# Start-up fills, first loads and delay terms of a planned two-layer kernel: one variant in place of another

## The chip, the cores and the metric

One core of one Trainium2 chip runs the whole program. The metric is the device time of one execution in microseconds (us): the median of several runs. A run of this kernel is told from another at about 0.2%, some 3.7 us.

The core has five instruction streams that run beside each other and wait for each other through semaphores: TensorE (PE in the profile: matmuls; PEld: its weight loads), VectorE (DVE), ScalarE (ACT), GpSimd (POOL) and SyncE (SP, which here only issues DMA transfers). Each stream is executed strictly in the order in which it was written.

## The reference, cut to what matters

Two layers are applied twice in turn to x (2048 tokens x 512): A is attention over segments of 32 tokens with a memory of 8 tokens that is handed from segment to segment, B is a gated feed-forward layer. Both passes use the same weights.

```
def _A_ref(x, mem0, Wq, Wk, Wv, Wo, seg_len):     # 32 heads of 128, M = 8
    mem = mem0
    for s in range(n_seg):                         # 64 segments of 32 tokens
        h = concatenate([mem, x[segment s]])       # 40 rows
        q, k, v = h @ Wq, h @ Wk, h @ Wv           # per head
        p = softmax(where(mask, q @ k.T * scale, -1e9))
        o = (p @ v) summed over heads through Wo
        mem = o[:, :M]                             # memory of the next segment
        outs.append(o[:, M:])
def _B_ref(x, w_gate, w_up, w_down):
    return (sigmoid(x @ w_gate) * (x @ w_up)) @ w_down
x = x + _A_ref(_layernorm(x), ...)
x = x + _B_ref(_layernorm(x), ...)
x = x + _A_ref(_layernorm(x), ...)
x = x + _B_ref(_layernorm(x), ...)
```

Segment s+1 needs the memory that segment s leaves, so layer A is a chain of 64 steps; the feed-forward layer and the V projections of tokens that are already known hang on no such chain.

## The kernel before, in words

**Steps.** The kernel runs 70 steps (`emit_step`). Step t treats segment t of the first pass of layer A (job 0) and segment t-6 of the second pass (job 1) together, where both exist: steps 0 to 5 have job 0 alone (40 rows), steps 6 to 63 have both (80 rows), steps 64 to 69 have job 1 alone. In a step the 32 heads go in units of 3 heads and groups of 6 (the last of 2). For each unit: Q and K by matmuls with `wq`, `wk` (L721), a copy to `qku`, scores (L735). For each group: the softmax (L748 to L780: mask, maximum, subtraction, exponential on ACT, sum, reciprocal, product into `pb`), a transpose by matmul (L794), a copy to `ptsb`, P times V (L807), a copy to `otsb`, Wo (L824). After the last head the 8 memory rows go into `hT` of the next step (L837, or L842 with one job).

**V.** V of the x tokens is made ahead in passes of 128 rows (`v_pass`, L583): eight pieces of 512 columns, copied to a staging tile and stored to a scratch tensor in DRAM (`scr`); each step loads its 24 rows from there (L681). A store with fewer than 24 tokens per segment is rearranged so that the token is its outermost dimension (8 or 16) and the segment the next. The remaining 32 rows of each step (the memory and the newest tokens) are projected in the step itself (`add_strips`, L693), copied in two halves to `sst`, and moved to `vsb` by four DMAs (L702). Nine V passes, 288 matmuls of 512 columns, belong to the start (`v_group`); the others come with the feed-forward blocks.

**Start.** `setup_consts` makes the identity, the masks and small constants. `clear` plans the zero fills of `hT`, `pb` and `vsb` and the small `maskb` transfer. Then come the loads of x blocks, of the initial memory (`load_mem0`) and of the weights (`load_weights`), about 18 MB. Layer norm (`layernorm_T`) is on DVE except for the power -1/2, which POOL computes (L542).

**What sets the order.** All work is entered as tasks with an engine, a duration and what it reads and writes (`Planner.add`). `plan` orders the tasks of each engine by list scheduling with these durations, with a latency from each engine to those that wait for it (`gap`), and with places in rotating buffers; it also chooses between ACT and DVE for tasks that name both. `late` adds a term to the latency from a TensorE task to the task that has it: -980 ns for the copy of the first strip half, +40 ns for the `qku` copy, +240 ns for the copy into `oxT`. The order found is then written out. So a change of an assumed duration or latency can move instructions anywhere in the program. Early loads carry a `boost` that sets their order; the SP queue waits, at each DMA, for the DMA eight places earlier.

Of the kernel before, what the change touches and what calls it, by code (L numbers as in the profile page):

```python
# [16 lines left out]
P = 128  # L17
MEM = 8
SEG = 32
L = MEM + SEG  # L20
LW = 2 * L
# [5 lines left out]
BLK = 4  # L27
# [24 lines left out]
class Task:  # L52
    __slots__ = ("eng", "dur", "lat", "fn", "deps", "succ", "tail", "boost", "ndep", "ready", "start", "idx", "on", "fresh", "acq", "rel", "durs", "tick", "prev", "land", "adj")

    def __init__(self, eng, dur, lat, fn, boost):
        self.durs = dur if isinstance(dur, dict) else {e: dur for e in eng}
        self.eng, self.dur, self.lat, self.fn, self.boost = eng, min(self.durs.values()), lat, fn, boost
        self.deps, self.succ, self.fresh = set(), [], set()
        self.acq, self.rel = [], []
        self.on = None  # L60
        self.land = 3000.0
        self.adj = {}
# [21 lines left out]
class Planner:  # L84
# [18 lines left out]
    def add(self, eng, dur, fn, r=(), w=(), lat=None, boost=0.0, use=(), late=0.0):  # L103
# [18 lines left out]
        if late:  # L122
            tk.adj = {d: late for d in tk.fresh if self.tasks[d].eng == ("PE",)}
# [6 lines left out]
    def gap(self, a, b):  # L130

        d = b.adj.get(a.idx, 0.0)
        if a.eng == b.eng:
            return a.lat if a.eng[0] in ("DVE", "ACT", "SP") or len(a.eng) > 1 else 0.0
        return a.lat + d + (self.TO_PE if b.eng[0] == "PE" else 0.0)
# [211 lines left out]
class Kern:  # L347
# [103 lines left out]
    def setup_consts(self):  # L451
        nc, tc = self.nc, self.tc
        cmasks.make_identity(nc, self.ident[:])
# [5 lines left out]
        nc.gpsimd.memset(self.mask1[0:MEM, :], 0.0)  # L459
        nc.gpsimd.affine_select(out=self.maskb[0:L, 0:SEG], in_=self.maskb[0:L, 0:SEG], pattern=[[-1, SEG]],  # L460
# [6 lines left out]

    def clear(self):

        nc, pl = self.nc, self.pl  # L470
        pl.add("SP", 430, lambda: nc.sync.dma_start(out=self.maskb[L:LW, :], in_=self.mask1[:]), w=["maskb"])
        for k, t_ in enumerate(self.hT):
            pl.add("DVE", 120, lambda t_=t_: nc.vector.memset(t_[:, :, L:2 * L], 0.0), w=[("hT", k, 1, q) for q in ("m", "x")])
        for k, t_ in enumerate(self.pb):
            pl.add("DVE", 400, lambda t_=t_: nc.vector.memset(t_[:], 0.0), w=[("pb", k)])
        for k, t_ in enumerate(self.vsb):
            keys = [("vs", k), ("vx", 0, k), ("vx", 1, k)]
            if k == 0:
                pl.add("DVE", 550, lambda t_=t_: nc.vector.memset(t_[:], 0.0), w=keys)
            else:  # L480
                pl.add("ACT", 960, lambda t_=t_: nc.scalar.copy(out=t_[:], in_=self.vsb[0][:]), r=[("vs", 0)], w=keys)

    def load_weights(self):
# [9 lines left out]
        xb = list(self.boot_x)[1:]  # L493
        for h0, n in ((0, 4), (4, 4), (8, 8), (16, 8), (24, 8)):
            cs = slice(h0 * P, (h0 + n) * P)
            ld(self.wv[:, :, cs], wv_v[:, :, cs], P * self.DC * n * P * 2 / 300.0, [("wv", h) for h in range(h0, h0 + n)])
            if h0 == 0:
                continue
            for b in xb[:3]:
                self.load_x(b, *self.boot_x[b])  # L500
            xb = xb[3:]
        for g, (h0, gsz, us) in enumerate(self.groups):
            cs = slice(h0 * P, (h0 + gsz) * P)
            nb = P * self.DC * gsz * P * 2
            for nm, sb, v in (("wq", self.wq, wq_v), ("wk", self.wk, wk_v)):
                ld(sb[:, :, cs], v[:, :, cs], nb / 300.0, [(nm, h) for h in range(h0, h0 + gsz)])
            ld(self.wo[:, h0:h0 + gsz, :], wo_v[:, h0:h0 + gsz, :], P * gsz * self.D * 2 / 300.0, [("wo", h) for h in range(h0, h0 + gsz)])
# [6 lines left out]
    def load_mem0(self):  # L514
        nc, pl, DC = self.nc, self.pl, self.DC
        m0 = self.xo[0][0:MEM, :]
        pl.add("SP", 100, lambda: nc.sync.dma_start(out=m0, in_=self.mem0), w=[("xo", 0)], lat=2500.0, boost=self.boot())
# [114 lines left out]
    def pre1(self, b):  # L632
        nc, pl = self.nc, self.pl
        i = self.nxt("xs", self.NX)
        xb = self.xs[i]
        pl.add("SP", 430, lambda: nc.sync.dma_start(out=xb[:], in_=self.x_in[b * P:(b + 1) * P, :]), w=[("xs", i)], lat=2500.0 if b < 2 else None, boost=(self.boot() if b < 2 else 0))
# [12 lines left out]
    def emit_step(self, t):  # L649
# [34 lines left out]
        def add_strips(col, lo, key):  # L684
# [13 lines left out]
            for q in range(2):  # L698
                pl.add(("ACT", "DVE"), copy_ns(512), lambda q=q: (sb[:, q, :], vb[q][:, :]), r=[vb[q]], w=[(sb, q)], use=[sb], late=-980.0 * (q == 0))
# [7 lines left out]
        for g, (h0, gsz, us) in enumerate(self.groups):  # L707
            hs = slice(0, gsz)
            SB = pl.buf(self.bank)
            for u in us:  # L710
# [20 lines left out]
                pl.add("ACT", act_ns(2 * nh * ncol, True), qkcopy, r=[pq], w=[qku], late=40.0)  # L731
# [12 lines left out]
            for idx, j in reversed(list(enumerate(jobs))):  # L744
# [6 lines left out]
                    r=[SB] + ([("st", gi, 0)] if both and j == 0 else []) + (["maskb"] if both else []), w=[("st", gi, 0), ("st", gi, 1)])  # L751
# [92 lines left out]
        for idx, j in enumerate(jobs):  # L844
# [4 lines left out]
            pl.add("ACT", 160, lambda dst=dst, a=48 * j - c0: (dst, wo3(a, SEG)), r=[WB], w=[("oxT", j, oi, s % BLK)], late=240.0)  # L849
# [120 lines left out]
    def trace(self):  # L970
        self.fill = {}
        self.lw = None
        self.clear()
# [7 lines left out]
        self.load_x(2, *self.boot_x[2])  # L981
        self.load_mem0()
# [20 lines left out]
    def run(self):  # L1003
        nc = self.nc
        self.setup_tiles()
        self.trace()
        order = self.pl.plan()
        with self.tc.manual_schedule():
            self.setup_consts()
# [67 lines left out]
```

## Time and profile before

| quantity | before |
|---|---|
| time, median of 3 runs | 1860.91 us (1858.97 to 1861.75) |
| profiled execution: time, span | 1860.91 us, 1859.1 us |
| PE busy | 1818.1 us (98%) |
| DVE, ACT, POOL busy | 1274.6 us (69%), 1173.8 us (63%), 571.8 us (31%) |
| granted TensorE clock, mean | 0.996 |
| HBM traffic over the span | 134 GB/s |

The profile describes one execution, of 1860.91 us, whose span between the first and the last instruction is 1859.1 us; 1.8 us lie around it. Busy time is the time in which an engine has at least one instruction running. Idle time of an engine is put down to what ended it ("<-"). Matmuls overlap in TensorE's pipeline, so the distance from one start to the next, not the length of one, is their cost.

### The profile page before, as it was taken

Reading aid. Unit: us, or ns where it says so; the run is one execution under the profiler, and the core shown is the slowest. Engines: PE = TensorE matmul, PEld = TensorE weight load, DVE = VectorE, ACT = ScalarE, POOL = GpSimd, SP = SyncE. Lnnn points to the kernel's source line nnn. Section 1 sums busy time; section 2 is a strip of 40 time slices with the busy share of each in tenths; the row PEclk is TensorE's granted clock in tenths of the full one; section 3 lists DMA queues with packets and bytes.
Section 4 is the critical chain, followed back from the end, with each engine's and each line's share of the span. In section 5 each row is a group of like instructions: output and inputs, shape, how many; then the busy total and the mean of one; then the engine's idle time right before and its main releaser. Section 6 shows DMA issues by size and latency. Waiting matters only on the chain.

```text
span 1859.1 us, 94041 instructions
## 1 busy us (share of the span) xinstructions
PE 1818.1 (98%) x41066; PEld 1577.1 (85%) x41282; DVE 1274.6 (69%) x4115; ACT 1173.8 (63%) x2748; POOL 571.8 (31%) x821
## 2 busy tenths in 40 slices
PE   7999999999999999999999999999999999999998
PEld 3678788889888898989888888989888888988787
DVE  5456566776677667767677777767677666767565
ACT  6665666666666666666666656666666666665553
POOL 4215023322424142323424142323424142324223
PEclk9999999999999999999999999999999999999999
DMA  9626234444645454554645364554645454545434
GB/s 354 229 77 175 69 101 139 138 146 131 174 130 169 117 168 124 153 150 132 177 129 168 101 183 122 150 153 129 181 129 166 115 163 125 156 135 165 140 96 135
DMA packets 128438, 273.79 MB, mean 147 GB/s; under 512 B 26882, under 2 KB 59402, under 8 KB 128026
## 3 DMA queue, kind: packets, MB, share of 16 engines
q0 software_dynamic: 56848, 183.48, 33.4%
q1 hardware_dynamic: 71178, 84.29, 15.9%
q8 instruction: 323, 5.29, 1.2%
q14 instruction: 89, 0.73, 0.1%
HBM read 221.85 MB, written 27.26 MB: 134 GB/s over the span
## 4 chain that ended last, share of the span: by engine, by line
PE 94%; DVE 2%; ACT 2%; issue 1%; DMA 1%; POOL 0%; SPq 0%; ACTq 0%; DVEq 0%; POOLq 0%
PE bank L721 33%; PE bank L824 16%; PE bank L923 11%; PE bank L583 9%; PE bank L693 7%; PE bank L735 5%; PE bank L794 4%; PE bank L807 4%; PE bank L947 4%; PE bank L552 1%; DMA vsb<-sst 0%; PE bank L891 0%; ACT otsb L1017 0%; ACT ptsb L1017 0%; DVE ptsb L1019 0%
## 5 line engine op out<-in xcount | busy, mean ns | idle before, releaser
L721 PE MATMUL bank<-hT,wq_sb 128*128 128x80 bf16 (+1 forms) x8960 | 622.1, 198 | 2.7 <-ACT hT L1017 0.7
L721 PE MATMUL bank<-hT,wk_sb 128*128 128x80 bf16 (+1 forms) x8960 | 621.4, 198 | 0.8 <-issue 0.7
L1017 ACT CAST qku<-bank 128x480 bf16<-128x480 f32 (+3 forms) x770 | 394.5, 512 | 251.2 <-PE bank L721 224.1
L721 PEld LDWEIGHTS <-wq_sb 128*128 128x128 bf16 x8960 | 458.6, 99 | 27.5 <-DVE hT L837 3.5
L721 PEld LDWEIGHTS <-wk_sb 128*128 128x128 bf16 x8960 | 450.6, 99 | 1.2 <-issue 1.0
L748 DVE TENSOR_TENSOR st<-bank,maskb 80x240 f32<-80x240 f32 (+1 forms) x732 | 269.8, 370 | 223.1 <-PE bank L735 211.2
L824 PE MATMUL bank<-otsb,wo_sb 128*128 128x80 bf16 (+1 forms) x8960 | 368.0, 198 | 7.0 <-ACT otsb L1017 3.7
L824 PEld LDWEIGHTS <-wo_sb 128*128 128x128 bf16 x8960 | 339.2, 99 | 23.9 <-issue 6.9
L915 POOL DMA_DIRECT2D wg<-in_B_w_gate_dram x217 | 165.2, 762 | 493.8 <-PE bank L923 440.3
L1017 ACT CAST otsb<-bank 128x480 bf16<-128x480 f32 (+3 forms) x420 | 200.6, 487 | 92.2 <-PE bank L807 73.1
L777 DVE TENSOR_TENSOR pb<-st,rz 80x480 bf16<-80x480 f32 x348 | 206.4, 594 | 5.5 <-PE bank L794 0.3
L760 DVE TENSOR_REDUCE sm<-st 80x6 f32<-80x240 f32 (+3 forms) x420 | 153.4, 366 | 75.3 <-ACT st L758 73.2
L542 POOL TENSOR_TENSOR lns<-lns,negh 128x1 f32<-128x1 f32 (+1 forms) x79 | 44.3, 562 | 520.1 <-DVE lns L541 433.1
L941 POOL DMA_DIRECT2D wd<-in_B_w_down_dram x217 | 154.0, 712 | 157.1 <-PE bank L735 66.0
L1017 ACT CAST ptsb<-bank 128x480 bf16<-128x480 f32 (+3 forms) x321 | 158.7, 496 | 56.1 <-PE bank L794 53.0
L758 ACT ACTIVATE st<-st 80x240 f32<-80x240 f32 (+3 forms) x420 | 160.1, 382 | 32.1 <-DVE st L755 31.2
L923 PE MATMUL bank<-xnT,wg 128*128 128x128 bf16 (+2 forms) x1784 | 173.0, 219 | 2.6 <-ACT xnT L1017 1.6
L923 PE MATMUL bank<-xnT,wu 128*128 128x128 bf16 (+2 forms) x1784 | 171.9, 219 | 0.0
L916 POOL DMA_DIRECT2D wu<-in_B_w_up_dram x217 | 162.7, 750 | 6.4 <-PE bank L923 2.2
L735 PE MATMUL bank<-qku 128*80 128x80 bf16 (+1 forms) x2240 | 163.0, 202 | 1.4 <-ACT qku L1017 0.3
L755 DVE TENSOR_TENSOR st<-st,mx 80x240 f32<-80x240 f32 (+3 forms) x420 | 156.0, 371 | 5.0
L735 PEld LDWEIGHTS <-qku 128*80 128x80 bf16 (+1 forms) x2240 | 123.6, 117 | 42.0 <-ACT sst L1017 22.1
(99 smaller groups left out, 2463.5 us busy)
## 6 DMA issues: line engine op xcount, KB each, us to landing
wg<-in_B_w_gate_dram POOLq DMA_DIRECT2D x220, 256.0 KB, 4.2
wu<-in_B_w_up_dram POOLq DMA_DIRECT2D x220, 256.0 KB, 4.7
wd<-in_B_w_down_dram POOLq DMA_DIRECT2D x220, 256.0 KB, 5.2
vsb<-scr SPq DMA_DIRECT2D x508, 48.0 KB
vsb<-sst SPq DMA_DIRECT2D x280, 64.0 KB
scr<-vst SPq DMA_DIRECT2D x128, 96.0 KB
wq_sb<-in_A_Wq_dram SPq DMA_DIRECT2D x5, 768.0 KB
wk_sb<-in_A_Wk_dram SPq DMA_DIRECT2D x5, 768.0 KB
```

The source lines that it names most:

```text
L583: nc.tensor.matmul(B[:, :], lhsT=tile[:, c, :], rhs=self.wv[:, c, cs], start=(c == 0), stop=(c == DC - 1))
L721: nc.tensor.matmul(o_ap, lhsT=W[:, c, h * P:(h + 1) * P], rhs=mv(c), start=(c == 0), stop=(c == DC - 1))
L735: nc.tensor.matmul(s_all(SB)[pr, uh - h0 + i, :], lhsT=qku[:, i, 0, 0:ncol], rhs=qku[:, i, 1, 0:ncol], start=True, stop=True)
L748: pl.add("DVE", dve_ns(n, True), lambda gsz=gsz, hs=hs, st=st, SB=SB, pj_=pj_, npj_=npj_, mk=mk, idx=idx: nc.vector.tensor_tensor(out=st[p ...
L755: pl.add("DVE", dve_ns(n), lambda gsz=gsz, hs=hs, st=st, mx=mx: nc.vector.tensor_tensor(out=st[pr, hs], in0=st[pr, hs], in1=mx[pr, hs].uns ...
L758: pl.add("ACT", act_ns(n), lambda hs=hs, st=st: nc.scalar.activation(out=st[pr, hs], in_=st[pr, hs], func=ACTF.Exp, scale=self.scale), r=s ...
L777: nc.vector.tensor_tensor(out=o, in0=st[pr, hs].unsqueeze(1).to_broadcast([npart, 2, gsz, L]), in1=rz[pr, :, 0:gsz].unsqueeze(3).to_broadc ...
L824: nc.tensor.matmul(WB[:, c * ncol:(c + 1) * ncol], lhsT=self.wo[:, h, c * P:(c + 1) * P], rhs=otsb[:, hl, 0:ncol], start=(h == 0 and c == ...
L915: pl.add("POOL", 760, lambda wg=wg, fs=fs: nc.gpsimd.dma_start(out=wg[:], in_=self.wgv[:, :, fs]), r=[("wo", self.H - 1)], w=[gk] + bt, la ...
L916: pl.add("POOL", 760, lambda wu=wu, fs=fs: nc.gpsimd.dma_start(out=wu[:], in_=self.wuv[:, :, fs]), r=[("wo", self.H - 1)], w=[uk] + bt, la ...
L923: nc.tensor.matmul(gu[:, 2 * i + k, 0:n], lhsT=W[:, c, i * P:(i + 1) * P], rhs=xnT[:, c, rw], start=(c == 0), stop=(c == DC - 1))
L1017: nc.scalar.copy(out=dst, in_=src)
```

## The change

The changed kernel differs in these points; the V passes, the form of the V stores, the steps and the feed-forward layer have the same code.

- The zero fills of `hT` and `pb` are written ahead of the plan, in `setup_consts`, on DVE. The five fills of `vsb` (before: one on DVE, and four copies of it on ACT) are five planned memsets on POOL. The identity is made in float32 in the tile `st` and copied to bf16 on DVE. `maskb` is loaded right after its mask is made.
- The initial memory is loaded first, then x blocks 0 and 1, then the first quarter of `wv` (1 MB in place of two transfers of 512 KB), then x block 2.
- The planner takes the loads of `wq` and `wk` at 260 and of `wo` at 200 bytes per ns (before 300), takes the usual 4000 ns in place of 2500 ns for the first loads, and has no `late` terms.

```diff
     def gap(self, a, b):
-        d = b.adj.get(a.idx, 0.0)
...
-        return a.lat + d + (self.TO_PE if b.eng[0] == "PE" else 0.0)
+        return a.lat + (self.TO_PE if b.eng[0] == "PE" else 0.0)
...
     def setup_consts(self):
-        cmasks.make_identity(nc, self.ident[:])
+        identf = fview(self.st[1][:, 0, 0:1], [(1, P)])
+        cmasks.make_identity(nc, identf)
+        nc.vector.tensor_copy(out=self.ident[:], in_=identf)
...
+        nc.sync.dma_start(out=self.maskb[L:LW, :], in_=self.mask1[:])
...
-    def clear(self):
-        pl.add("SP", 430, lambda: nc.sync.dma_start(out=self.maskb[L:LW, :], in_=self.mask1[:]), w=["maskb"])
-        for k, t_ in enumerate(self.hT):
-            pl.add("DVE", 120, lambda t_=t_: nc.vector.memset(t_[:, :, L:2 * L], 0.0), w=[("hT", k, 1, q) for q in ("m", "x")])
-        for k, t_ in enumerate(self.pb):
-            pl.add("DVE", 400, lambda t_=t_: nc.vector.memset(t_[:], 0.0), w=[("pb", k)])
+        for t_ in self.hT:
+            nc.vector.memset(t_[:, :, L:2 * L], 0.0)
+        for t_ in self.pb:
+            nc.vector.memset(t_[:], 0.0)
         for k, t_ in enumerate(self.vsb):
-            keys = [("vs", k), ("vx", 0, k), ("vx", 1, k)]
-            if k == 0:
-                pl.add("DVE", 550, lambda t_=t_: nc.vector.memset(t_[:], 0.0), w=keys)
-            else:
-                pl.add("ACT", 960, lambda t_=t_: nc.scalar.copy(out=t_[:], in_=self.vsb[0][:]), r=[("vs", 0)], w=keys)
+            self.pl.add("POOL", 950, lambda t_=t_: nc.gpsimd.memset(t_[:], 0.0), w=[("vs", k), ("vx", 0, k), ("vx", 1, k)])
...
     def load_weights(self):
-        for h0, n in ((0, 4), (4, 4), (8, 8), (16, 8), (24, 8)):
+        for h0 in range(0, self.H, 8):
...
-                ld(sb[:, :, cs], v[:, :, cs], nb / 300.0, [(nm, h) for h in range(h0, h0 + gsz)])
-            ld(self.wo[:, h0:h0 + gsz, :], wo_v[:, h0:h0 + gsz, :], P * gsz * self.D * 2 / 300.0, [("wo", h) for h in range(h0, h0 + gsz)])
+                ld(sb[:, :, cs], v[:, :, cs], nb / 260.0, [(nm, h) for h in range(h0, h0 + gsz)])
+            ld(self.wo[:, h0:h0 + gsz, :], wo_v[:, h0:h0 + gsz, :], P * gsz * self.D * 2 / 200.0, [("wo", h) for h in range(h0, h0 + gsz)])
...
-                pl.add(("ACT", "DVE"), copy_ns(512), lambda q=q: (sb[:, q, :], vb[q][:, :]), r=[vb[q]], w=[(sb, q)], use=[sb], late=-980.0 * (q == 0))
+                pl.add(("ACT", "DVE"), copy_ns(512), lambda q=q: (sb[:, q, :], vb[q][:, :]), r=[vb[q]], w=[(sb, q)], use=[sb])
...
-                pl.add("ACT", act_ns(2 * nh * ncol, True), qkcopy, r=[pq], w=[qku], late=40.0)
+                pl.add("ACT", act_ns(2 * nh * ncol, True), qkcopy, r=[pq], w=[qku])
...
-            pl.add("ACT", 160, lambda dst=dst, a=48 * j - c0: (dst, wo3(a, SEG)), r=[WB], w=[("oxT", j, oi, s % BLK)], late=240.0)
+            pl.add("ACT", 160, lambda dst=dst, a=48 * j - c0: (dst, wo3(a, SEG)), r=[WB], w=[("oxT", j, oi, s % BLK)])
...
     def trace(self):
-        self.clear()
+        self.load_mem0()
         p0 = self.pre1(0)
         p1 = self.pre1(1)
...
-        self.load_x(2, *self.boot_x[2])
-        self.load_mem0()
         self.load_weights()
...
     def run(self):
         self.setup_tiles()
+        self.setup_consts()
         self.trace()
         order = self.pl.plan()
         with self.tc.manual_schedule():
-            self.setup_consts()
```

## The prediction

> **What bounds the kernel now.** I read the page's first lines, then the chain that ended last, then busy time by stage. In the page, PE is busy for 98% of the span and is 94% of the chain.
>
> ```profile
> span 1859.1 us, 94041 instructions
> ...
> PE 1818.1 (98%) x41066; PEld 1577.1 (85%) x41282; DVE 1274.6 (69%) x4115; ACT 1173.8 (63%) x2748; POOL 571.8 (31%) x821
> ...
> PE 94%; DVE 2%; ACT 2%; issue 1%; DMA 1%; POOL 0%; SPq 0%; ACTq 0%; DVEq 0%; POOLq 0%
> ```
>
> Busy time by stage (length, then PE, PEld, DVE, ACT, POOL with their counts, granted clock, DMA share, GB/s):
>
> ```profile
> 0.00:8.77 8.77, 1.48 (x13) 0.87 (x13) 6.26 (x32) 6.59 (x10) 2.97 (x14) 1.00 0.72 228
> 8.77:16.20 7.43, 5.55 (x24) 2.22 (x25) 4.72 (x15) 2.88 (x6) 2.57 (x5) 1.00 1.06 380
> 93.00:140.00 47.00, 46.20 (x1112) 34.92 (x1116) 25.67 (x86) 29.47 (x81) 5.05 (x10) 1.00 0.27 76
> 465.00:930.00 465.00, 459.41 (x10365) 409.82 (x10422) 332.36 (x1069) 301.47 (x691) 151.72 (x211) 1.00 0.52 149
> ```
>
> Of 41.0 us in which PE idles, 9.2 lie in the first 16.2 us; between 465 and 930 us it idles 5.6. The number of matmuls is the same in both kernels, so the time moves only by PE's idle time and by small gaps between groups of matmuls. What a matmul costs is read from the chain in order of time: 72 of 40 columns in 1.90 us (26.4 ns each), 72 of 80 in 2.58 (35.9 ns); 24 of 512 columns lie 5.18 us in the chain (215.5 ns).
>
> ```profile
> 20.07 5.18 PE bank L583 x24
> ...
> 79.56 1.90 PE bank L721 x72
> ...
> 533.24 2.58 PE bank L721 x72
> ```
>
> **The start.** The timeline of the start, rows of three engines:
>
> ```profile
> 0.30 0.11 POOL L1058 MEMSET const-bfloat16-1.0<- 128x1 bf16 x1
> 0.73 0.21 POOL masks.py:197 MEMSET ident<- 128x128 bf16 x1 [0.29 <-POOLq L1058]
> ...
> 2.94 3.88 ACT L481 COPY vsb<-vsb 128x1024 bf16<-128x1024 bf16 x4 [0.92 <-DVE vsb L479]
> ...
> 5.30 1.07 POOL L542 TENSOR_TENSOR lns<-lns,negh 128x1 f32<-128x1 f32 x2 [3.20 <-DVE lns L541]
> ...
> 8.77 1.89 PE L583 MATMUL bank<-wv_sb,xvf 128*128 128x512 bf16 x4 [0.62 <-ACT xvf L1017]
> ```
>
> POOL's set-up ends at 2.10 us, and the first powers (L542) begin at 5.30, when DVE has their input. In the compiled order of the changed kernel the five vsb memsets stand on POOL ahead of that power. Price of one (128 x 1024 bf16, not in the trace): two POOL memset rows give 0.11 us for 1 element and 0.21 for 128, 0.79 ns an element, so 0.92 us. Ends: 0.48 (DVE's vsb memset) and 1.56 (the slope of POOL's affine_select, 0.29 us at 128). I take 0.92, the same operation on the same engine: five are 4.6 us, POOL is free at 6.7, and the first power, normalisation, transpose and V matmul come 1.4 us later, at 10.2 to 10.3. Behind the power on POOL wait those of blocks 1 and 2; behind the maskb transfer, now ninth on SP, x blocks 5, 7 and 8 and the third quarter of wv, but its mask is ready near 4 us, before SP gets there.
>
> Only a part of the 1.4 us stays, because PE idles again in the kernel before, 1.58 us ahead of block 3's transpose at 15.99. In the changed order DVE does block 2's statistics only after block 1's pieces: xvf copy 10.3 to 11.0, statistics of blocks 2, 3 and 4 (0.65 each) to 12.95, power to 13.65, normalisation (0.41) to 14.1, transpose, ACT copy to 15.3. PE has two pieces of V (8 matmuls) until then and runs on from 15.35. At 16.2 us it has done 12 V matmuls against 16: 4 x 0.2155 = **+0.9 us**. Ends: -0.6 (memset at 0.48, POOL early, DVE rid of its own 0.48) and +4.0 (memset at 1.56, POOL free at 9.9, power 4.6 later). The 1 MB piece of wv is no new wait: with blocks 0 and 1 it is 1.25 MB, some 4 to 5.5 us at the 380 and 228 GB/s of the stages, before 10 us. ACT loses 3.88 us of copies that ended at 6.82, before its first copy of the chain at 7.00: nothing on the path. The identity's copy (some 0.2 us on DVE, bound 0.5) ends before 3.6, when the initial memory's transposes need it: nothing.
>
> A rule that speaks against putting fills on POOL is in the Trainium skill, SBUF — State Buffer, "Who interferes with whom": DVE copies in a two-port mode and GpSimd lock each other out. The trace shows POOL's set-up undisturbed (0.73 to 2.10) beside DVE's memsets from 0.81 to 3.63. By the rule the identity copy and two memory copies, some 0.5 us, would come on top, and the start would cost +1.2.
>
> **Steps 0 to 5.** The slower assumed weight loads move step 0's end behind 260 V matmuls, against 212 in the order before; 48 x 0.2155 = 10.3 us. By itself this costs nothing: PE does the same V work sooner. What is late next: only 28 of the 288 early V matmuls remain to fill steps 1 to 5, against 76. Priced by the rows above, steps 2 and 3 have 16.7 and 14.8 us of TensorE work instead of 21.5 and 20.4.
>
> I measured in both compiled orders how much TensorE work lies between a producer and its consumer, and compared it with what the trace shows must lie between:
>
> ```profile
> 126.05 0.36 ACT L1017 CAST qku<-bank 128x240 bf16<-128x240 f32 x1 [0.30 <-PE bank L721]
> ...
> 1316.97 0.56 ACT L1017 CAST qku<-bank 128x480 bf16<-128x480 f32 x1 [0.30 <-PE bank L721]
> ```
>
> QK to scores: 0.30 wait + 0.36 copy = 0.66 us with 40 rows, 0.30 + 0.56 + 0.04 = 0.90 with 80. In the same way transpose to PV 0.72 and 0.90, PV to Wo 0.66 and 0.90, Wo to the next QK 0.52 and 0.60, scores to transpose 3.2 (31.9 to 35.1 us in step 0) and 4.2, strips to PV 4.3; the last, small group less. Where the work is less than that, PE stands still for the rest. Sums of these shortfalls, before to changed: steps 0 to 5, 2.3 to 6.4 us; steps 64 to 69, 4.1 to 4.8.
>
> **Steps 6 to 63.** Without the +40 ns the planner puts scores right behind 24 QK matmuls (24 x 35.9 = 0.86 us, under 0.90): 55 units stand so, against 11. QK to scores: 0.2 to 2.0 us of shortfall; transpose to PV 1.7 to 3.8; PV to Wo 6.3 to 8.4; scores to transpose 0.3 to 1.1; strips 0.9 to 1.1; Wo to QK 1.6 to 1.1. Sum 10.8 to 17.5.
>
> All shortfalls: 17.2 to 28.7, +11.5. Two that follow each other in one group overlap, which in the extreme halves it (5.8). On the other side PE idles 28.6 us between 16.2 us and its end where the shortfalls of before make 17.2, so the method may see only 60%: 19. I take **+8.5**, three quarters, since most of the new ones stand in neighbouring links of the same groups.
>
> **Small groups with 40 rows.** In the timeline, six score matmuls last until the next group 0.26 us, three 0.18, where 26.4 ns each would be 0.16 and 0.08: each visit costs 0.10.
>
> ```profile
> 83.48 0.32 PE L735 MATMUL bank<-qku 128*40 128x40 bf16 x6
> 83.74 0.27 PE L721 MATMUL bank<-hT,wq_sb 128*128 128x40 bf16 x4
> ...
> 85.64 0.25 PE L735 MATMUL bank<-qku 128*40 128x40 bf16 x3
> 85.82 0.27 PE L721 MATMUL bank<-hT,wq_sb 128*128 128x40 bf16 x4
> ```
>
> The changed order has 165 such visits (scores and transposes), before 149: **+1.6 us**. With 80 rows (464 score groups against 406) the trace shows no such cost: three last 0.11, six 0.23.
>
> **Copies that change engine.** 53 PSUM copies move from ACT to DVE, 44 of them the second half of the strips (0.59 us on ACT, 0.71 on DVE). DVE's 69% becomes some 71%; the strips' DMAs have more room in the order than before. Price 0, between -3.2 (all PE waits for those DMAs gone) and +2 (half of the 0.12 x 53 and its queueing on the path).
>
> **Sum.** 0.9 + 8.5 + 1.6 = +11.0 us. The profiled execution is itself the median, 1860.9 us (span 1859.1 and 1.8 around it): **1872 us**.
>
> **Rivals.** (a) *The order's gaps do not bite*: the shortfalls are tens of ns each, and PE's queue hides them; then 0.9 + 1.6 = +2.5, 1863.4, not told from no change. Against it: the order before has the 4.3 us strip link short by 0.85 in step 6, and PE waited 1.4 us there. (b) *Faster by a lighter ACT*: PE's waits for ACT and for the strips' DMA are these, of all the profile lists:
>
> ```profile
> PE bank L824 <- ACT otsb L1017: 3.7, 8, 0.7
> PE bank L807 <- DMA vsb<-sst: 3.0, 5, 1.4
> ```
>
> With xnT 1.6, hT 0.7, xvf 0.6 and qku 0.3 they are 9.9 us. ACT loses 57 copies; if all these waits go and no new gap bites, 1860.9 - 9.9 + 2.5 = 1853.5. It decides once the relief exceeds some 11 us plus 3.7, or the gaps are nothing. Against it: ACT is idle 37% of the span, so its waits come from the order, not from load. (c) *POOL is slower*: memset at 1.56, start +4.0: 1875. (d) *DVE becomes the bound of the bare steps*: a group takes 5 x 0.40 + 0.18 = 2.2 us of DVE, 11.7 a step, with copies some 13 of the 14.8 us; if queueing adds 2 us in each of steps 2 to 4, 1878. (e) *The stated change does nothing*: the V stores have 8 or 16 as outermost dimension in both orders, 24 and 24 of each in the start; price 0 in every case. The Trainium skill, DMA: Bandwidth & Descriptors, "Why a DMA increments its semaphore by 16 and not by 1", lets that dimension choose the number of DMA engines; no run here shows it, and by it too the sum stays.
>
> **How the numbers follow.** Forecast 0.55, (a) 0.12, (b) 0.05, (c) 0.13, (d) 0.15. The lower end, 1862, is case (a) less half of its spread; the upper, 1884, is the start at +4.0 with shortfalls of 19 (+24.6 in all is 1885.5). 0.2% is 3.7 us, about what can be told. Faster 0.06, within 0.11, slower 0.83.
>
> **What would show it.** First power on POOL near 6.7 us and first V matmul near 10.3; 16 us into the span some 0.9 us more PE idle; first PV matmul some 11 us later than 70.5; several waits of PE for qku, ptsb and otsb between 100 and 165 us; PE idle between 465 and 930 us of some 7 to 8 us; span 1870. Wrong: PE idle there unchanged or less, or a DMA as the longest wait of PE after 70 us.

## The result, and the profile after

The changed kernel takes 1873.01 us (median of 4 runs, 1870.35 to 1873.84), the kernel before 1861.33 us (4 runs, 1858.97 to 1861.92): a ratio of 1.0063, 95% interval 1.0045 to 1.008, or +11.7 us. 1872 was forecast. The number is right; the experiments below show that a good part of the reasons is not.

The first lines of the changed kernel's page (span, busy time of each engine, shares of the chain that ended last):

```profile
span 1868.6 us, 94264 instructions
...
PE 1824.7 (98%) x41085; PEld 1579.3 (85%) x41282; DVE 1294.5 (69%) x4168; ACT 1143.7 (61%) x2691; POOL 586.3 (31%) x832
...
PE 92%; DVE 4%; ACT 2%; issue 1%; DMA 1%; SPq 0%; POOL 0%; ACTq 0%; DVEq 0%
```

PE is busy 6.6 us longer than before with the same matmuls. They did not become dearer in the steady state: in the chain, 72 matmuls of 80 columns still take 2.58 us. Up to 4.1 us of the 6.6 are a matter of records: this trace lacks 197 matmuls of 512 columns (PE x41085 beside PEld x41282) and that of before 216 (x41066), and time in which a matmul is not recorded counts as idle. What is sure is that part of the loss is busy time in which the same work runs slower; the section on the granted clock shows it. The profiled execution is the fastest of the four, 1870.35 us, so its trace holds 9.4 of the 11.7 us.

Busy time by stage, in the stretches shown of before (length, PE, PEld, DVE, ACT, POOL with counts, granted clock, DMA share, GB/s):

```profile
0.00:8.77 8.77, 0.24 (x4) 0.25 (x4) 7.32 (x25) 1.28 (x1) 6.01 (x17) 1.00 0.75 244
8.77:16.20 7.43, 5.24 (x20) 1.99 (x20) 4.78 (x16) 3.44 (x11) 2.33 (x5) 1.00 1.07 372
93.00:140.00 47.00, 45.52 (x1280) 37.21 (x1279) 29.14 (x98) 27.96 (x83) 9.25 (x14) 1.00 0.34 97
465.00:930.00 465.00, 461.02 (x10401) 410.43 (x10448) 340.21 (x1096) 294.02 (x677) 157.01 (x215) 1.00 0.52 149
```

The reader is to see two things. In the first 16.2 us PE idles 10.7 us instead of 9.2. Between 465 and 930 us, where 7 to 8 us were expected, it idles 4.0 us, less than the 5.6 of before. Most of both is matmuls without a record. Two runs described below have all records; there the order of before (with POOL memsets added) and the changed one (with both sets of idle matmuls) idle 1.55 and 1.63 us in this stretch:

```profile
465.00:930.00 465.00, 463.45 (x10455) 410.85 (x10453) 333.43 (x1071) 302.07 (x692) 152.26 (x212) 1.00 0.53 149
465.00:930.00 465.00, 463.37 (x10452) 410.41 (x10448) 340.17 (x1096) 293.48 (x676) 156.71 (x215) 1.00 0.52 149
```

A row of the chain, the waits of PE, and the copy and the scores of one unit in the changed kernel:

```profile
205.04 2.58 PE bank L709 x72
```

```profile
PE bank L513 <- DVE ident L451: 6.4, 1, 6.4
PE bank L540 <- DVE xn L531: 5.9, 6, 2.8
PE bank L795 <- DMA vsb<-sst: 3.0, 5, 1.3
PE bank L812 <- ACT otsb L1003: 1.9, 5, 0.5
...
PE bank L723 <- ACT qku L1003: 0.2, 1, 0.2
```

```profile
229.72 0.56 ACT L1003 CAST qku<-bank 128x480 bf16<-128x480 f32 x1 [0.27 <-PE bank L709]
...
230.38 0.28 PE L723 MATMUL bank<-qku 128*80 128x80 bf16 x3
```

Between the QK matmuls of this unit and its scores (L723) lie only the 24 QK matmuls of the next unit, 24 x 35.9 ns = 0.86 us; the scores start 0.10 us after the copy has ended, and PE does not wait. The trace has 55 such units in steps 6 to 63, and that of before 11, as the prediction counted them. In 53 of the 55 the scores start 0.90 to 0.92 us after the last QK matmul of their unit started, which is 0.86 us and the spacing of one matmul; none has PE idle ahead of its scores. In the waits qku, said to be late, has 0.2 us in one place (0.3 before); the identity (6.4 us) is new, and otsb is down from 3.7 to 1.9.

**Where the time went.** For each step I took its end (the start of VectorE's copy of the new memory into `hT`) and subtracted the TensorE work done by then, each matmul at its steady spacing (215.5 ns for 512 columns, 35.9 for 80, 26.4 for 40, and so on). What is left grows only by stalls and slow stretches; it is worked out from the timelines and good to about 1 us.

| left over at the end of step, us | 0 | 5 | 6 | 10 | 20 | 62 | 68 |
|---|---|---|---|---|---|---|---|
| before | 14.1 | 24.2 | 28.6 | 33.9 | 39.9 | 54.6 | 67.7 |
| changed | 17.7 | 33.2 | 39.4 | 44.8 | 49.6 | 65.7 | 78.3 |
| delay terms taken away alone | 14.8 | 28.4 | 32.1 | 39.1 | 43.9 | 60.6 | 72.6 |
| slower assumed loads alone | 14.8 | 32.6 | 37.0 | 41.7 | 46.6 | 62.0 | 73.1 |
| changed start alone | 16.3 | 26.2 | 29.6 | 34.1 | 39.8 | 54.6 | 65.4 |
| POOL memsets added alone | 15.8 | 25.8 | 30.3 | 34.9 | 39.9 | 55.7 | 66.4 |

The changed kernel loses 3.6 us by the end of step 0, 5.4 in steps 1 to 5, 1.8 in step 6, and then nothing: the difference is 10.8 us at step 6 and 10.6 at step 68.

### The profile page after: what moved, and what is told of

Its sections match the earlier page's. It is cut to its first block, busy times and chain, and to the rows that moved or that the text cites. A ratio compares the mean times of both kernels' runs of the same rounds, so it can differ in the third digit from the quotient of the medians.

```text
span 1868.6 us, 94264 instructions
## 1 busy us (share of the span) xinstructions
PE 1824.7 (98%) x41085; PEld 1579.3 (85%) x41282; DVE 1294.5 (69%) x4168; ACT 1143.7 (61%) x2691; POOL 586.3 (31%) x832
## 3 DMA queue, kind: packets, MB, share of 16 engines
q1 hardware_dynamic: 70010, 83.17, 15.5%
## 4 chain that ended last, share of the span: by engine, by line
PE 92%; DVE 4%; ACT 2%; issue 1%; DMA 1%; SPq 0%; POOL 0%; ACTq 0%; DVEq 0%
PE bank L709 32%; PE bank L812 16%; PE bank L911 11%; PE bank L571 9%; PE bank L681 7%; PE bank L723 5%; PE bank L935 4%; PE bank L782 4%; PE bank L795 4%; PE bank L540 1%; DVE pb L765 1%; ACT otsb L1003 1%; DVE st L736 0%; DVE lns L527 0%; DVE sm L748 0%
## 5 line engine op out<-in xcount | busy, mean ns | idle before, releaser
L812 PE MATMUL bank<-otsb,wo_sb 128*128 128x80 bf16 (+1 forms) x8960 | 375.8, 198 | 4.1 <-ACT otsb L1003 1.9
L530 POOL TENSOR_TENSOR lns<-lns,negh 128x1 f32<-128x1 f32 (+1 forms) x79 | 51.1, 648 | 502.3 <-DVE lns L529 445.3
L746 ACT ACTIVATE st<-st 80x240 f32<-80x240 f32 (+3 forms) x420 | 160.4, 382 | 60.6 <-DVE st L743 59.2
L1003 ACT CAST ptsb<-bank 128x480 bf16<-128x480 f32 (+3 forms) x300 | 147.6, 501 | 55.5 <-PE bank L782 54.1
L723 PE MATMUL bank<-qku 128*80 128x80 bf16 (+1 forms) x2240 | 175.7, 203 | 1.3 <-ACT qku L1003 0.2
L723 PEld LDWEIGHTS <-qku 128*80 128x80 bf16 (+1 forms) x2240 | 127.2, 117 | 44.7 <-ACT st L746 17.8
```

Of the source, the lines that this page charges most:

```text
L723: nc.tensor.matmul(s_all(SB)[pr, uh - h0 + i, :], lhsT=qku[:, i, 0, 0:ncol], rhs=qku[:, i, 1, 0:ncol], start=True, stop=True)
L746: pl.add("ACT", act_ns(n), lambda hs=hs, st=st: nc.scalar.activation(out=st[pr, hs], in_=st[pr, hs], func=ACTF.Exp, scale=self.scale), r=s ...
L812: nc.tensor.matmul(WB[:, c * ncol:(c + 1) * ncol], lhsT=self.wo[:, h, c * P:(c + 1) * P], rhs=otsb[:, hl, 0:ncol], start=(h == 0 and c == ...
L1003: nc.scalar.copy(out=dst, in_=src)
```

## The experiments

All were timed beside the kernel before; a difference in us is the ratio's excess times 1860, with the interval in brackets. Each part of the change was first run alone.

### The start

The timeline of the changed kernel's start:

```profile
1.01 0.94 POOL L471 MEMSET vsb<- 128x1024 bf16 x1
...
2.62 0.94 POOL L471 MEMSET vsb<- 128x1024 bf16 x1
3.00 3.38 DVE L451 CAST ident<-st 128x128 bf16<-128x128 f32 x1
...
3.57 2.73 POOL L471 MEMSET vsb<- 128x1024 bf16 x3
6.44 0.24 PE L513 MATMUL bank<-ident,xo 8*128 8x8 bf16 x4 [6.44 <-DVE ident L451]
...
8.44 1.08 POOL L530 TENSOR_TENSOR lns<-lns,negh 128x1 f32<-128x1 f32 x2 [2.14 <-DVE lns L528]
...
11.82 3.60 PE L571 MATMUL bank<-wv_sb,xvf 128*128 128x512 bf16 x8 [0.53 <-DMA xa<-in_A_x_dram]
```

A memset takes 0.94 us (0.92 was estimated) and POOL is free at 6.30. But VectorE's copy of the identity, priced at 0.2 us, lasts 3.38: it begins beside the second memset and ends 0.08 us after the last. Everything behind it on DVE waits, and the first V matmul comes at 11.82, not 10.3. To test this, the copy alone was moved to ScalarE in the changed kernel:

```diff
-        nc.vector.tensor_copy(out=self.ident[:], in_=identf)
+        nc.scalar.copy(out=self.ident[:], in_=identf)
```

> The changed kernel with one instruction moved: the float32 to bf16 copy of the identity is done by ScalarE in place of VectorE; every other instruction and the order on every engine are those of the changed kernel. In its trace that copy took 3.38 us on VectorE (3.00 to 6.38 us), and POOL's last three vsb memsets ran from 3.57 to 6.30. Theory A (VectorE's cast is held up by the POOL memsets): on ScalarE the copy takes well under 1 us and ends near 3 us, VectorE's first statistics start near 4 us and not 6.81, the first power waits for POOL until 6.3 to 6.4 us, the first V matmul starts near 9.7 us and not 11.82, and the span is 1.5 to 2 us shorter than the changed kernel's 1868.6. Rival (the copy is slow by itself, or waits for something that any engine would wait for): it ends near 6.4 us again, and nothing changes.

```profile
2.36 0.30 ACT L451 CAST ident<-st 128x128 bf16<-128x128 f32 x1 [0.34 <-POOL st masks.py:199]
...
9.66 3.60 PE L571 MATMUL bank<-wv_sb,xvf 128*128 128x512 bf16 x8 [0.53 <-ACT xvf L1003]
14.66 4.35 PE L571 MATMUL bank<-wv_sb,xvf 128*128 128x512 bf16 x12 [0.81 <-ACT xvf L1003]
```

On ACT the copy takes 0.30 us, and the first V matmul comes 2.16 us earlier. The time is 1869.47 us, +8.4 us against before (6.1 to 10.6), which the changed kernel's +11.7 (8.4 to 14.9) does not exclude. In the trace hardly anything of the 2.16 us lives on: the next twelve V matmuls, 2.76 us in the changed kernel, now take 4.35, and step 0 ends at 90.6 us instead of 91.1. The reason is the clock: the first V matmuls start 0.427 us apart, later ones 0.2155, and the trace's first clock record begins where the spacing changes, at 17.9 us here, 15.5 in the changed kernel and 12.0 in the kernel before. So the blocked cast is shown; that it costs the end anything is not.

Next, the kernel before with the changed start alone (fills, identity, `maskb`, order and assumed latency of the first loads), the delay terms and 300 bytes per ns kept:

```diff
-        self.clear()
+        self.load_mem0()
...
-        cmasks.make_identity(nc, self.ident[:])
+        nc.vector.tensor_copy(out=self.ident[:], in_=identf)
...
+            self.pl.add("POOL", 950, lambda t_=t_: nc.gpsimd.memset(t_[:], 0.0), w=[("vs", k), ("vx", 0, k), ("vx", 1, k)])
```

> The kernel before with only the start of the changed one: fills on POOL, identity in float32 with its copy on VectorE, the order of the first loads and their assumed 4000 ns; delay terms and rates as before. Step 0 ends behind 212 V matmuls as before. Theory: the first V matmul near 11.8 us, step 0 ends 3 to 4 us later than in before, and the time is 3 to 4 us longer, no more. Rival (the 1.5 to 2 us that the blocked copy costs are swallowed by work that waits for weights): step 0 ends within 1 us of before, and so does the kernel.

1859.87 us, -0.9 us (-2.4 to +0.6): no difference, although the trace has the same cast and the same first V matmul, and step 0 ends 2.2 us later than in before:

```profile
3.00 3.38 DVE L455 CAST ident<-st 128x128 bf16<-128x128 f32 x1
6.43 0.25 PE L517 MATMUL bank<-ident,xo 8*128 8x8 bf16 x4 [6.43 <-DVE ident L455]
11.82 3.16 PE L575 MATMUL bank<-wv_sb,xvf 128*128 128x512 bf16 x8 [0.53 <-ACT xvf L1007]
```

Since this kernel is also planned anew, the delay was made once more with the order of before untouched:

```diff
+        for t_ in self.vsb:
+            nc.gpsimd.memset(t_[:], 0.0)
         nc.vector.memset(self.negh[:], -0.5)
```

> The kernel before with five more memsets of the vsb tiles (128 x 1024, measured 0.94 us each in the changed kernel) ahead of everything else that POOL fills, 4.7 us of POOL work in front of the first power; each engine's planned order is untouched, so TensorE has the same 212 V matmuls in step 0. The first power begins near 6.8 us instead of 5.30 and the first V matmul near 10.3 instead of 8.77 (later, up to 11.8, if VectorE's memsets are held up beside POOL's). Theory that a late start passes through to the end: 1.5 to 3 us slower, 1861.5 to 1863 against 1860. Rival, from the run with the changed start alone (2.2 us behind at the end of step 0, level with before at step 10): the delay meets later waits that end at a fixed time (for weights) and is gone by step 10; no difference over 1 us.

```profile
2.04 4.52 POOL L463 MEMSET vsb<- 128x1024 bf16 x5
...
3.62 0.76 DVE L475 MEMSET hT<- 128x80 uint32 x8
...
4.41 1.29 DVE L541 BATCH_NORM_STATS2 lns<-xs 128x6 f32<-128x512 bf16 x2
...
6.53 1.08 POOL L544 TENSOR_TENSOR lns<-lns,negh 128x1 f32<-128x1 f32 x2
```

The first V matmul comes at 10.57 us, 1.80 late, and the time is 1861.19 us, +1.1 us (-0.4 to +2.8), between the two theories and not told from nothing. Its row of the table, of one execution, the fastest of eleven, says more: 1.7 us behind at the end of step 0, 1.0 at step 10, level at step 20, and within some 1 us of before from there on. The rows above add that VectorE's memsets and statistics keep the length of before (0.76 and 1.29 us) beside POOL's memsets. It is the cast that was locked out.

### The delay terms

```diff
-                ... (sb[:, q, :], vb[q][:, :]), r=[vb[q]], w=[(sb, q)], use=[sb], late=-980.0 * (q == 0))
+                ... (sb[:, q, :], vb[q][:, :]), r=[vb[q]], w=[(sb, q)], use=[sb])
...
-                pl.add("ACT", act_ns(2 * nh * ncol, True), qkcopy, r=[pq], w=[qku], late=40.0)
+                pl.add("ACT", act_ns(2 * nh * ncol, True), qkcopy, r=[pq], w=[qku])
...
-            pl.add("ACT", 160, ..., late=240.0)
+            pl.add("ACT", 160, ...)
```

> The kernel before with the three delay terms of the planner removed (-980 ns for the first strip half, +40 ns for the qku copy, +240 ns for the oxT copy); start and load rates are those of before. The prediction's term (gaps of tens of ns between QK and scores and their like): 5 to 6.6 us slower over steps 6 to 63, with more PE idle time between 465 and 1740 us than the 12.1 us before. Rival, which the trace of the changed kernel suggests (its idle time there is 10.7 us): no change, within 2 us of before, and the order of steps 6 to 63 costs nothing.

1867.94 us, +7.3 us (4.7 to 9.7): the largest part. But the table puts it into steps 0 to 10 (5.2 us by step 10, 4.9 at step 68). Which term it is was asked by taking away one at a time (the lines above, the second alone and the first alone):

> The kernel before without one delay term, the +40 ns on the qku copy; the terms of -980 ns (strip copy) and +240 ns (oxT copy) stay. All three taken away cost +6.8 us, all of it in steps 0 to 10. Theory of the prediction, that scores right behind 24 QK matmuls are what costs: 1865 to 1868, with PE waits for qku. Rival, that this link is long enough and the loss comes from the order that the strip term sets: 1860 to 1862, no PE wait for qku over 1 us.

1862.32 us, +2.4 us (0.4 to 4.3), and PE waits for qku 0.3 us in one place, as in before. The time lies between the two ranges; 48 units stand right behind 24 QK matmuls here and none makes PE wait, so the prediction's link is not the cause.

> The kernel before without the term of -980 ns on the first strip half; the +40 ns and +240 ns stay. Theory that the strip term makes the loss of 6.8 us: 1866 to 1868, with more idle time of PE in steps 1 to 10 than before. Rival, the qku term: 1860 to 1862. If this and the run without the +40 ns both lose 2 to 4 us, any other order of the first steps is worse than that of before, and no single link is the cause.

1865.25 us, +5.0 us (3.3 to 6.9). Both lose, and the two together make the 7.3 us of all three, so no single link is the cause; the order found without either term is worse. Nor is there one place: in its profile the run without -980 ns is 2.2 us behind at step 10, level at step 20, and loses 4 us between steps 47 and 62. The third term was not taken away by itself.

### The assumed rates of the weight loads

```diff
-                ld(sb[:, :, cs], v[:, :, cs], nb / 300.0, [(nm, h) for h in range(h0, h0 + gsz)])
+                ld(sb[:, :, cs], v[:, :, cs], nb / 260.0, [(nm, h) for h in range(h0, h0 + gsz)])
...      and wo: / 300.0 becomes / 200.0
```

> The kernel before with only the planner's assumed rates changed: 260 for wq and wk and 200 for wo in place of 300. Step 0 then ends behind 256 of the early V matmuls, against 212, and 32 are left for steps 1 to 5. Theory (bare steps leave PE idle or at a lower clock): step 0 ends some 9 us later, which costs nothing, and by the end of step 6 the order has lost 4 to 7 us more than before; the time is 4 to 7 us longer, and stays so to the end. Rival (the loss between 77 and 230 us in the changed kernel is only the late start and a clock dip that falls there by chance): within 1.5 us of before.

1865.95 us, +4.7 us (2.6 to 6.7); in its profile it is 8.4 us behind at the end of step 6, more than expected, and 5.4 at step 68. Then the changed kernel with this part undone, and the rates moved the other way (360 for all) in the kernel before:

> The changed kernel with the assumed weight loads back at 300 bytes per ns; the changed start stays and there are no delay terms. The three parts alone measured -1.2 (start), +6.8 (delay terms), +4.8 us (rates) against the kernel before, +11.9 all together. If the parts add: about 1867 us (1866 to 1868), with 1 to 3 us more over the priced TensorE work than before by step 10 from the rates gone. If the rates lose only beside the missing delay terms or the late start, the gain here is larger: 1861 to 1865. If the rates cost nothing once the delay terms are gone: 1872 to 1874. A granted clock without dips between 140 and 260 us goes with the first two, dips with the third.

1865.42 us, +6.1 us (3.9 to 8.4), as the parts added give. The two signs named with it missed: the profile is some 7 us behind at step 10, not 1 to 3, and has a half clock from 192.6 to 196.0 us. Alone they are -0.9, +7.3 and +4.7, together 11.1 of the 11.7 us.

> The kernel before with all weight loads assumed at 360 bytes per ns, the other direction of the rate term: step 0 then ends behind 180 V matmuls and leaves 108 as fill for steps 1 to 5 (before: 212 and 76; 260 and 200 bytes per ns: 256 and 32, which measured +4.8 us). Theory that missing fill in the first steps costs the time, in proportion: 32/44 of 4.8 the other way, 3 to 4 us faster, 1857 to 1858. Rival, saturation: in the kernel before the clock shows no dip in these steps, so more fill adds nothing: 1860 to 1862. Rival, transfers: the weights land when they land, and the first QK and Wo matmuls of step 0 then wait for them on the path, with fewer V matmuls ahead of them: up to 32 x 0.2155 = 6.9 us, 1864 to 1868.

1867.39 us, +6.9 us (4.3 to 9.5). More fill left for steps 1 to 5 does not help: by the measure of the table some 5 us are lost by the end of step 0 and about 1 more in steps 1 to 5. Step 0 starts its first QK too early and waits for a weight (2.7 us in the row below), the third theory:

```profile
PE bank L721 <- DMA wk_sb<-in_A_Wk_dram: 2.7, 2, 1.7
```

### The granted clock

In its profile, the kernel with the slower rates has a granted clock of 0.66 from 140 to 160 us: 6.8 us lost there, and the kernel before none. The changed kernel in stretches of 4 us, and PE's timeline where steps 5 and 6 meet:

```profile
140.00:144.00 4.00, 3.65 (x103) 3.15 (x100) 3.24 (x12) 3.14 (x11) 0.00 (x0) 1.00 0.28 66
144.00:148.00 4.00, 4.00 (x115) 3.72 (x111) 2.51 (x11) 2.20 (x7) 0.00 (x0) 0.65 0.15 41
148.00:152.00 4.00, 3.69 (x98) 3.51 (x96) 0.63 (x3) 1.21 (x4) 0.00 (x0) 0.50 0.07 16
192.00:196.00 4.00, 2.13 (x60) 1.77 (x57) 1.29 (x5) 1.06 (x4) 3.10 (x5) 1.00 0.89 270
196.00:200.00 4.00, 3.25 (x53) 3.23 (x51) 0.58 (x2) 1.26 (x4) 0.00 (x0) 0.57 0.45 148
```

```profile
195.62 0.40 PE L540 MATMUL bank<-ident,xn 128*128 128x128 bf16 x4 [1.82 <-DVE xn L531]
196.77 0.42 PE L709 MATMUL bank<-hT,wq_sb 128*128 128x80 bf16 x4 [0.75 <-ACT hT L1003]
196.99 0.47 PE L709 MATMUL bank<-hT,wk_sb 128*128 128x80 bf16 x4
197.26 0.47 PE L709 MATMUL bank<-hT,wq_sb 128*128 128x80 bf16 x4
```

Behind 1.82 and 0.75 us of idle time four QK matmuls take 0.27 us from start to start, where 4 x 35.9 ns is 0.144: TensorE runs at about half speed for 3 us, and the profile calls that time busy. The Trainium skill, TensorE: Matmul & The Clock Gate, "Part 1: The HAM clock gate", has a clock that is either whole or half, set by how busy TensorE was in windows of some 3.4 us. The values 0.50 and 1.00 agree with it, and so do the half stretches of these traces, 3.41 us long or a multiple of it (the last, cut off by the end, aside).

To test whether the idle time brings the low clock, seven matmuls whose result nothing reads were put into that gap, in the bank that the waiting transposes overwrite:

```diff
         def tr():
+            for _ in range(warm):
+                nc.tensor.matmul(B[:, :], lhsT=self.ident[:], rhs=self.wv[:, 0, 0:512], start=True, stop=True)
...
-            pst2, B2 = self.layernorm_T(xo[:], ok)
+            pst2, B2 = self.layernorm_T(xo[:], ok, warm=7 if b == 0 else 0)
```

> The changed kernel with seven matmuls of 512 columns more, whose result nothing reads, in the gap of 1.82 us in which PE waits for xn between steps 5 and 6 (195.62 us); they go into the bank that the waiting transposes overwrite, and wait for nothing. 7 x 0.2155 = 1.5 us, inside the gap. Theory that idle time bunched in a few us brings the half clock that follows (0.57 from 196 to 200 us, where four QK matmuls take 0.265 us in place of 0.143): the clock stays at 1.00 there, and the time falls by 1.5 to 2 us against the changed kernel, to about 1869 on a chip where before is 1860. Rival, that the low clock is set by the many small matmuls before the gap or by something else: the clock falls as before and the time is that of the changed kernel, about 1871, or 0.3 us more.

```profile
195.35 1.67 PE L540 MATMUL bank<-wv_sb,ident 128*128 128x512 bf16 x7
197.31 0.40 PE L542 MATMUL bank<-ident,xn 128*128 128x128 bf16 x4 [0.29 <-DVE xn L531]
198.45 0.30 PE L711 MATMUL bank<-hT,wq_sb 128*128 128x80 bf16 x4 [0.75 <-ACT hT L1005]
198.59 0.31 PE L711 MATMUL bank<-hT,wk_sb 128*128 128x80 bf16 x4
```

With the gap filled the QK matmuls run at full speed (0.14 us for four) and step 6, 32.6 us long in the changed kernel, takes 30.8: 1.8 us, as expected. The whole is 1868.72 us, +10.2 us (8.0 to 12.5) against before, 1.5 less than the changed kernel, which the intervals don't separate. In this profile the dip of step 3 stays (146.5 to 153.3 us), and one comes at 245.5 us that the changed kernel's profile has not; the run with the identity on ScalarE has one at 246.6. So which places fall differs between executions of one TensorE order.

Step 3 has no such gap (its longest wait in that stretch is 0.34 us), but in the changed kernel no V matmul either: all 288 are done when step 2 ends. Twelve more idle matmuls went there, two ahead of each group's transposes:

```diff
                 def ptr(gsz=gsz, pb=pb, PB=PB):
+                    for _ in range(2 if t == 3 else 0):
+                        nc.tensor.matmul(PB[:, :], lhsT=self.ident[:], rhs=self.wv[:, 0, 0:512], start=True, stop=True)
```

> The changed kernel with the seven idle matmuls of the gap at 195 us as in the run before, and two more of 512 columns ahead of the transposes of each of the six groups of step 3 (141 to 148 us), in the bank that these transposes overwrite: 12 x 0.2155 = 2.6 us of work that does nothing. In the changed kernel the clock is 0.83 from 140 to 160 us, 3.4 us lost. Theory that step 3 falls to the half clock because it has no wide matmul of V left among its narrow ones: the clock stays at 1.00 from 136 to 156 us, and 3.4 - 2.6 = 0.8 us are won: about 1868 where before is 1860. Rival, that other work or the chip sets that dip: the clock falls as before and 2.6 us are added: 1871 to 1872.

```profile
132.00:136.00 4.00, 4.00 (x119) 3.81 (x115) 1.13 (x3) 1.40 (x4) 4.00 (x7) 0.57 0.95 289
...
144.00:148.00 4.00, 3.69 (x93) 2.62 (x90) 3.13 (x12) 2.41 (x9) 0.00 (x0) 1.00 0.07 16
148.00:152.00 4.00, 3.85 (x100) 2.77 (x96) 0.62 (x3) 1.99 (x8) 0.00 (x0) 1.00 0.10 25
```

The clock stays at 1.00 from 136 to 156 us (a smaller dip came at 132), and over its five runs the mean clock is 0.9978, against 0.9945 in the changed kernel. The time, 1870.11 us, +10.6 (8.0 to 13.2), is not better than with the seven: the 2.6 us of idle matmuls cost what they bring. So more TensorE work at these two places keeps the clock whole there: one profile each shows it, and the mean clock of the runs agrees (0.9945 over four runs, 0.9962 over six with the seven, 0.9978 over five with all). Which measure of activity sets the clock is not shown, and neither is a use of it.

Last, the same in reverse: the kernel before, its order untouched, with most of the V fill behind step 0 left out:

```diff
-                for c in range(DC):
-                    nc.tensor.matmul(B[:, :], lhsT=tile[:, c, :], rhs=self.wv[:, c, cs], start=(c == 0), stop=(c == DC - 1))
+                self.vdone = getattr(self, "vdone", 0) + boot
+                nc_ = 1 if boot and self.vdone > 53 else DC
+                for c in range(nc_):
+                    nc.tensor.matmul(B[:, :], lhsT=tile[:, c, :], rhs=self.wv[:, c, cs], start=(c == 0), stop=(c == nc_ - 1))
```

> The kernel before, but the last 19 of the 72 V pieces of the start, all of those that come after step 0, run one of their four matmuls only (so V of these rows is a quarter of its sum): 57 matmuls of 512 columns are left out, 57 x 0.2155 = 12.3 us of TensorE work, and the order of everything else is untouched. If that fill is only work, the time falls by 12.3 us, to 1848. Theory that it covers the links between the small matmuls of steps 1 to 5 and keeps the granted clock up: PE idles more between 80 and 190 us, the granted clock falls to half for some us there, and the time falls by 5 to 8 us only, to 1852 to 1855.

```profile
144.00:148.00 4.00, 2.34 (x76) 2.09 (x73) 2.27 (x8) 1.79 (x6) 1.50 (x2) 1.00 0.90 253
148.00:152.00 4.00, 3.46 (x58) 2.63 (x59) 2.17 (x7) 1.45 (x5) 0.70 (x1) 0.59 0.06 18
```

1849.51 us, -10.2 us (-12.5 to -8.0), of 12.3 that were left out. The bare steps do idle and do fall to the half clock in the profile (3.4 us in 140 to 160), but in all only some 2 us of the saving are lost (by the interval none to 4), not the 4 to 7 expected. So fill is mostly work and a little cover; its absence does not explain the 11.7 us by itself.

**The clock in the balance.** The mean granted clock over the runs is 0.997 for before, 0.9945 for the changed kernel, 0.9944 for the slower rates alone, 0.9957 without the delay terms, 0.9971 for the start alone. Times 1865, 0.0025 is 4.7 us: counted in full, about 5 us of the +11.7 are the lower clock and about 7 us order. So counted, the slower rates' +4.7 us are all clock (0.0026 x 1865 = 4.8); of the delay terms' +7.3, 2.4 are. The run with both sets of idle matmuls agrees: its clock is no lower than before's (0.9978 against 0.9971 beside it), and +10.6 less 19 x 0.2155 = 4.1 us of idle matmuls leaves 6.5. But in the 72 runs of before that stand beside the experiments the time rises by only 1.0 us (standard error 0.13) with each 0.001 of clock, not 1.9; by that the clock is 2.5 of the 11.7 us. Its share is bounded to some 2.5 to 5 us, no closer.

## Why the prediction was right, and where it was not

- **The sum, +11.0, against +11.7**: right by luck, through errors that cancel.
- **A term that is not in the sum: the clock.** That "the time moves only by PE's idle time and by small gaps between groups of matmuls" failed: 2.5 to 5 of the 11.7 us are matmuls that run at half clock and count as busy.
- **The start, +0.9 (-0.6 to +4.0)**: too low at its place, nothing at the end. "The identity's copy (some 0.2 us on DVE, bound 0.5) ends before 3.6" failed: 3.38 us, to 6.38. The rule was cited for it, the Trainium skill's SBUF — State Buffer, "Who interferes with whom", with +0.3 us as its price; the direction was right, and the size was that of four memsets, because the copy did not get in between them. The two memory copies to which the prediction stretched the rule read PSUM and were not held (0.16 to 0.17 us beside POOL's memsets, 0.17 in before). The memset's 0.92 us (measured 0.94) and POOL's end at 6.7 (6.3) held. The V matmuls of the start were priced at 0.2155 us where they take 0.427; at 16.2 us 8 are done against 16, not 12. Then 3.6 us of delay at step 0 should have passed on; alone, it was taken up by waits of the first twenty steps. Whether it is also taken up beside the other two parts is open: the lead of 10.8 us at step 6 holds all of it and can't be split.
- **Steps 0 to 5, shortfalls of 4.1, taken as 3.1**: right in place, low in size. Steps 1 to 5 lost 5.4 us, of which 3.4 are clock (6.83 us at 0.50 in steps 3 and 4), which no row of before hints at in these steps.
- **Steps 6 to 63, +6.7, taken as 5.0: the step that failed.** From step 6 to 62 the difference moves by 0.3 us. QK to scores had 1.8 of the 6.7: the 0.90 us asked for there is too long, the 0.04 added to the trace's 0.30 and 0.56 is not there, and 0.86 is what 24 matmuls fill exactly (55 units, none waits). The links from transpose to PV and from PV to Wo had 4.2, and these do bite: below, with four transposes (0.22 us of work) between them, Wo starts 0.91 us after the last PV matmul started (745.08), right behind the copy. What failed is that the sum took only what gets worse. In steps 7 to 62 PE's waits for pb and ptsb rise from 0.5 to 2.3 us, and those for otsb and xnT fall from 3.8 to 1.0. The wrong sign that was named, "PE idle there unchanged or less", came: 4.0 us, and unchanged where all matmuls are on record. The 28.6 us of idle time, beside which the shortfalls of before made only 17.2, were a matter of records too: the same order with all of them (POOL memsets added) idles 16.9 us there.

```profile
744.90 0.38 PE L795 MATMUL bank<-ptsb,vsb 128*128 128x80 bf16 x6
745.38 0.56 ACT L1003 CAST otsb<-bank 128x480 bf16<-128x480 f32 x1
745.53 0.40 PE L540 MATMUL bank<-ident,xn 128*128 128x128 bf16 x4 [0.24 <-DVE xn L531]
745.99 0.59 PE L812 MATMUL bank<-otsb,wo_sb 128*128 128x80 bf16 x12
```

- **Steps 64 to 69, +0.7, taken as 0.5**: nothing there; the difference falls by 0.5 us between steps 62 and 68.
- **Small groups, +1.6**: not seen apart. Without idle time and clock, what is left of steps 3 to 5 is 4.5 us against 5.2 of before, so nothing speaks for it.
- **Copies that change engine, 0**: right; PE's wait for the strips' DMA is 3.0 us in five places in both kernels.
- **Rivals.** (a), gaps that don't bite, was right about the sum of steps 6 to 63, though not about its reason, and wrong about steps 1 to 6. (c) fell (0.94 us a memset), and so did (d): steps 2 to 4 lost 3.5 us more than before (9.7 against 6.2 left over), clock among them, not 6. (b) had its relief (otsb 3.7 to 1.9, xnT 1.6 to 0.6), and new waits ate it up. (e) was not tested, since the stores are the same in both orders.

## What to carry to other kernels

A link is only short if the trace's own numbers, with no margin added, exceed the work in it: 0.04 us too much in 55 links made 1.8 us of a loss that did not exist. A new order ends waits as well as making them, so count both before adding up. Compare idle times of two traces only after comparing their counts of matmul records. After a change to a planner's numbers, first ask where TensorE's idle time gathers within a few microseconds or where narrow matmuls run without wide ones, since the half clock that followed here cost as much again (1.7 us behind a gap of 1.82) and is booked as busy. A delay in a start can be gone by the end, as both runs with a late start show: run it alone before counting it.

## What the runs showed of the hardware

- A VectorE copy from float32 to bfloat16 in SBUF was held by POOL's memsets for 3.38 us, through three memsets that began after it, in each of the five traces that have it; on ACT, 0.64 us earlier, it took 0.30. Memsets and statistics on VectorE beside the same memsets were not held.
- The granted clock fell to 0.50 at 145.2 us in the changed kernel, with no idle gap over 0.34 us in the 14 us ahead of it and with matmuls of 40 columns alone in the last 7. The Trainium skill, TensorE: Matmul & The Clock Gate, "HAM oscillation — how this bites in real kernels", speaks of idle gaps of more than some 3.4 us; here far less is enough, which is nearer to its next section, "A second HAM failure mode: psum-queue depth-cycling", where many short idles do it. And it is not settled by idle time alone: before has this stretch, idle for half of it, with the clock whole in it and in the next 8 us:

```profile
208.00:212.00 4.00, 2.02 (x27) 1.10 (x25) 1.21 (x2) 2.29 (x5) 0.00 (x0) 1.00 0.25 60
```

- The first V matmuls of 512 columns start 0.427 us apart instead of 0.2155. The clock column shows 1.00 there because the traces have no clock record that early: the first begins where the spacing changes (at 12.0 us in before, 15.5 in the changed kernel), so an earlier start is partly spent at half speed.
